# Linear attention beside a gated FFN on one core: the state gram with its operands exchanged, and the state turned by DMA

## The chip, the cores and the metric

One core of one Trainium2 chip. The metric is the device time of one execution in microseconds (us), the median of several. Executions of one kernel agree mostly within 0.3%. A run is compared only with runs of the kernel before that were made in turns with it on the same chip. The sets of runs were timed on several chips, so the ratio to the kernel before, and not the bare median, compares one set with another. Runs with a lowered clock of TensorE throughout are set aside.

## The reference

Two branches over x (2048 tokens, 640 features) are mixed by a gate per token. Branch A is linear attention with 32 heads of 20 features. Its keys and queries go through a feature map of two softmaxes, so each head has 40 features: 20 of "plus" and 20 of "minus" sign.

```python
pk = einsum("bhsd,hdf->bhsf", k, w_phi)
phi_k = concatenate([softmax(pk), softmax(-pk)], axis=-1)      # and phi_q likewise
kv  = einsum("bhsf,bhsd->bhfd", phi_k, v)                      # the state, per head 40 x 20
z   = einsum("bhsf->bhf", phi_k)
num = einsum("bhqf,bhfd->bhqd", phi_q, kv)                     # the numerators
den = einsum("bhqf,bhf->bhq", phi_q, z) + 1e-6
a   = (num / den) @ wo
b   = (gelu(x @ w_gate) * (x @ w_up)) @ w_down                 # branch B, F = 1728
out = g * a + (1 - g) * b
```

The change concerns `kv` and `z`. v carries a column of ones for each head, so one matrix product gives both; it is called the state gram below.

## The kernel before

The kernel runs in three stages: loads and weight folding (to about 23 us), a loop over 16 blocks of 128 tokens that makes keys, values and queries and adds up the gram, and the FFN in four blocks of 512 tokens. The FFN makes the hidden layer in 14 chunks (numbered 0 to 13 in the order in which they run), then the down-projection. The program gives each engine one order of instructions, and semaphores tie the engines together.

A gram pass (one per token block) makes the 128 x 128 array hold 128 key features and streams the v columns (20 + 1 per head) of the heads that those features touch. Feature tiles of 128 do not end at head borders, so a tile touches 7 or 8 heads:

```python
def gram_regions(self):            # bank -> (sign, feature tile, first head, last head)
    ...
    return {
        3: [full(0, 0), full(0, 1), full(0, 3), (1, 2, 12, 14)],
        4: [full(1, 0), full(1, 1), full(1, 3), (1, 2, 15, 17)],
        5: [full(0, 4), full(1, 4), full(0, 2), (1, 2, 18, 19)],
    }

def gram(self, t):
    ...
    n = (h1 - h0 + 1) * self.DA                                   # DA = 21
    matmul(bank(b)[:, c:c + n], Ek[:, se, s, i*P:(i+1)*P], vaug[:, sv, h0:h1+1, :], ...)
```

That is 12 matmuls a pass, 8 with 147 streamed columns, one with 168, two with 63 and one with 42: 1512 columns. After the last pass 12 VectorE multiplies take the state out of PSUM, set what belongs to no head to zero with a mask, and write it as KV, with features on the partitions. The numerators need it in that layout. The first FFN block is woven with the last passes and the first numerators:

```python
order = [0, 1, 13] + list(range(2, 13))
at = {5: 0, 8: 1, 11: 2}             # after which chunk which numerator runs
for idx, c in enumerate(order):
    self.gateup(b, c, ...)           # one chunk: ten matmuls of 512 columns
    if idx == 0: self.gram(14)
    if idx == 3: self.gram(15); self.kv_evac(); self.gates()
    if idx in at: self.num(at[idx])
```

The softmax here doesn't subtract the row's maximum and nothing guards it: scores larger than these inputs give would overflow.

Of the kernel before, what the change touches and what calls it, by code (L numbers as in the profile page):

```python
# [3 lines left out]
P = 128  # L4
BF16 = mybir.dt.bfloat16
F32 = mybir.dt.float32
AF = mybir.ActivationFunctionType
ALU = mybir.AluOpType
# [95 lines left out]
class _Kernel:  # L104
# [353 lines left out]
            sc.op("dve", lambda e, v=v, r=r: e.tensor_tensor(v, v, r, ALU.mult),  # L458
                  reads=[("Rk", se)], writes=[("Ek", se, s)])

    def gram_regions(self):
        lo = self.HLO
        full = lambda s, i: (s, i, lo[i], self.HHI[i])
        return {
            3: [full(0, 0), full(0, 1), full(0, 3), (1, 2, 12, 14)],
            4: [full(1, 0), full(1, 1), full(1, 3), (1, 2, 15, 17)],
            5: [full(0, 4), full(1, 4), full(0, 2), (1, 2, 18, 19)],
        }

    def gram(self, t):  # L470
        sc = self.sc
        se, sv = t % self.NSE, t % self.NSV
        for b, regs in self.gram_regions().items():
            c = 0
            for r, (s, i, h0, h1) in enumerate(regs):
                n = (h1 - h0 + 1) * self.DA
                sc.op("pe", lambda e, s=s, i=i, h0=h0, h1=h1, c=c, n=n, b=b, r=r: e.matmul(  # L477
                    self.bank(b)[:, c:c + n], self.Ek[:, se, s, i * P:(i + 1) * P], self.vaug[:, sv, h0:h1 + 1, :],
                    start=(t == 0 and r == 0), stop=(t == self.NT - 1 and r == len(regs) - 1)),
                    reads=[("Ek", se, s), ("vaug", sv), ("vmain", sv), ("vone", sv)], writes=[("ps", b)],  # L480
                    signal=(r == len(regs) - 1))
                c += n

    def kv_evac(self):
        sc = self.sc
        for b, regs in self.gram_regions().items():
            c = 0
            for (s, i, h0, h1) in regs:
                nh = h1 - h0 + 1
                j0 = h0 - self.HLO[i]  # L490
                dst = self.KV[:, i, s, j0 * self.DB:(j0 + nh) * self.DB].rearrange(
                    "p (h c) -> p h c", c=self.DB)[:, :, 0:self.DA]
                src = self.bank(b)[:, c:c + nh * self.DA].rearrange("p (h c) -> p h c", c=self.DA)
                m = self.mask[:, i, j0:j0 + nh].unsqueeze(2).to_broadcast([P, nh, self.DA])
                sc.op("dve", lambda e, dst=dst, src=src, m=m: e.tensor_tensor(dst, src, m, ALU.mult),
                      reads=[("ps", b), ("mask", i), ("KVd", i, s)], writes=[("KV", i, s, h0)])
                c += nh * self.DA

    def pq(self, b, i, n):
        sc = self.sc  # L500
# [149 lines left out]
    def num(self, t):  # L650
        sc = self.sc
        NBK = self.NUMB
        DB, DH = self.DB, self.DH
        old = [("xtok", k) for k in range(4)] + [("wkT", g) for g in range(6)] + [("wqT", g) for g in range(6)]
        parts = {0: [(0, 0, 6), (1, 6, 12), (2, 12, 15)], 1: [(2, 16, 19), (3, 19, 25), (4, 25, 31)]}
        kvk = {(i, s): [] for i in range(5) for s in (0, 1)}
        for regs in self.gram_regions().values():
            for (s, i, h0, h1) in regs:
                kvk[(i, s)].append(("KV", i, s, h0))
        for hf in (0, 1):  # L660
            for s in (0, 1):
                bk = NBK + 2 * hf + s
                for r, (i, h0, h1) in enumerate(parts[hf]):
                    n = (h1 - h0 + 1) * DB
                    o0 = (h0 - 16 * hf) * DB
                    k0 = (h0 - self.HLO[i]) * DB
                    sc.op("pe", lambda e, s=s, i=i, n=n, o0=o0, k0=k0, bk=bk, r=r: e.matmul(  # L667
                        self.bank(bk)[:, o0:o0 + n], self.Eq[:, s, i, t * P:(t + 1) * P],
                        self.KV[:, i, s, k0:k0 + n], start=(r == 0), stop=(r == 2), skip_group_check=True),
                        reads=[("Eq", t // 4, s, i), ("KVd", i, s)] + kvk[(i, s)], writes=[("ps", bk)],  # L670
                        signal=(r == 2))
        sl = t % 2
        N = self.ps[:, NBK * 512:(NBK + 4) * 512].rearrange("p (f s c) -> p f s c", s=2, c=512)[:, :, :, 0:16 * DB]
        V = [N[:, :, s, :].rearrange("p f (h c) -> p f h c", c=DB) for s in (0, 1)]
        Z = [v[:, :, :, DH] for v in V]
        Dn = [v[:, :, :, DH + 1] for v in V]
        R = lambda k: self.RH[:, sl, k, :, :]
        rb = [("ps", NBK + k) for k in range(4)]
        key = lambda k: ("RH", sl, k)

        def dve(fn, reads, writes, guard=()):
            sc.op("dve", fn, reads=reads, writes=writes, guard=guard)
        dve(lambda e: e.reciprocal(R(0), Dn[1]), rb, [key(0)], guard=old)  # L683
        dve(lambda e: e.tensor_tensor(R(1), Dn[0], R(0), ALU.mult), rb + [key(0)], [key(1)])
        dve(lambda e: e.tensor_tensor(R(2), Z[1], R(1), ALU.mult), rb + [key(1)], [key(2)])
        dve(lambda e: e.tensor_tensor(R(3), Z[0], R(2), ALU.add), rb + [key(2)], [key(3)])
        dve(lambda e: e.scalar_tensor_tensor(R(4), Dn[0], 1e-6, R(3), ALU.mult, ALU.add), rb + [key(3)], [key(4)])
        dve(lambda e: e.reciprocal(R(5), R(4)), [key(4)], [key(5)])
        dve(lambda e: e.tensor_scalar(R(6), R(5), self.Gr[:, t:t + 1], None, op0=ALU.mult), [key(5), "Gr"], [key(6)])
        dve(lambda e: e.tensor_tensor(R(7), R(6), R(1), ALU.mult), [key(6), key(1)], [key(7)])  # L690
        for s, dst in ((0, self.O1), (1, self.O2)):
            o = dst[:, sl, :].rearrange("p (f h d) -> p f h d", f=2, d=DH)
            f = R(6 + s).unsqueeze(3).to_broadcast([P, 2, 16, DH])
            dve(lambda e, o=o, f=f, s=s: e.tensor_tensor(o, V[s][:, :, :, 0:DH], f, ALU.mult),  # L694
                rb + [key(6 + s)], [("O", s, sl)], guard=old)
        sc.op("pool", lambda e: e.tensor_tensor(self.Og[:, sl, :], self.O1[:, sl, :], self.O2[:, sl, :], ALU.add),  # L696
              reads=[("O", 0, sl), ("O", 1, sl)], writes=[("Og", sl)], guard=old)
        gs = t % 6
        sc.dma("sp", lambda e: e.dma_start_transpose(self.goT[:, gs, :, :], self.Og[:, sl, :]),
               reads=[("Og", sl)], writes=[("goT", gs)], guard=old)  # L700
# [49 lines left out]
    def ffn(self):  # L750
        self.gn = 0
        self.pn = 0
        self.sc.op("pool", lambda e: e.memset(self.hT[0:64, 13, :], 0.0), writes=["hTz"], guard=self.oldw)
        pairs = [(6, 7), (0, 1)]
        for b in range(self.NB):
            if b == 0:
                order = [0, 1, 13] + list(range(2, 13))
                at = {5: 0, 8: 1, 11: 2}
            else:
                order = list(range(14))  # L760
                at = {2: 4 * b + 1, 6: 4 * b + 2, 10: 4 * b + 3}
            for idx, c in enumerate(order):
                if b == 0 and c == 13:
                    self.gateup(b, c, (2,))
                else:
                    self.gateup(b, c, pairs[self.pn % 2])
                    self.pn += 1
                if b == 0:
                    if idx == 0:
                        self.gram(14)  # L770
                    if idx == 3:
                        self.gram(15)
                        self.kv_evac()
                        self.gates()
                if idx in at:
                    self.num(at[idx])
            for t in range(4):
                self.down(4 * b + t, pairs[self.pn % 2])
                self.pn += 1
                if b == 0 and t == 0:  # L780
                    self.num(3)
                if b < self.NB - 1 and t == 2:
                    self.num(4 * b + 4)
# [42 lines left out]
```

## Time and profile before

| | before |
|---|---|
| median | 306.58 us (306.54 to 307.19) |
| span in the profile | 304.5 us |
| TensorE / VectorE / ScalarE busy | 97% / 53% / 35% |
| one gram pass, start to start | 0.68 us, 16 times |

From the page of the kernel before: the busy times of the engines, the clock granted to TensorE in 40 slices of the span (9 is 90% or more of full speed), and the chain of work that ended last, by engine.

```profile
PE 296.6 (97%) x2002; PEld 175.0 (57%) x2028; DVE 162.3 (53%) x317; ACT 105.2 (35%) x186; POOL 30.0 (10%) x61
PEclk9999999999999999999999999999999999999999
PE 90%; SPq 4%; DMA 3%; ACT 1%; issue 1%; DVE 0%; DVEq 0%; ACTq 0%
```

PE is TensorE, PEld its weight loads. The chain is nine tenths matmul; the rest of it is the loading phase at the start. So what is taken from TensorE's stream after that phase comes off the time, as long as nothing new makes TensorE wait.

The gram's matmuls by shape (line, engine, operation, operands, count; busy us and mean ns of one; idle time before them):

```profile
L477 PEld LDWEIGHTS ps<-vaug,Ek 128*128 128x128 bf16 x192 | 12.3, 97 | 1.8
L477 PE MATMUL ps<-vaug,Ek 128*128 128x147 bf16 x128 | 11.8, 227 | 0.0
L477 PE MATMUL ps<-vaug,Ek 128*128 128x63 bf16 x32 | 6.1, 191 | 0.0
```

The means (227 ns, 191 ns) are latencies: matmuls overlap, and a mean says nothing about what one costs in a stream. The cost is the distance from one start to the next. From the records of one pass these are, in ns: 64, 68, 66, 28, 63, 68, 66, 28, 66, 63, 72, 28, in sum 680.

The chain of waits around the last pass, in order of time (start, length, what):

```profile
98.13 0.67 PE ps L477 x12
98.81 4.32 PE ps L630 x20
103.13 0.70 PE ps L667 x12
```

L477 is the gram, L630 the gate/up chunks, L667 the first numerator. They follow each other without a gap. Two chunks (4.32 us) lie between the last gram and the first numerator; in this time VectorE makes KV.

Three lines on DMA transposes in the kernel before, one of DMA issues (count, median us from issue to landing) and two of instructions (duration min/median/max in ns). xT is 512x640 from DRAM, goT 128x640 from SBUF:

```profile
xT<-in_A_x_dram SPq DMA_TRANSPOSE x3, 5.6
L228 SPq DMA_TRANSPOSE xT<-in_A_x_dram x3: 2677/2909/2956, 9.5 to 23.5; - x3
L699 SPq DMA_TRANSPOSE goT<-Og x16: 1200/1210/1241, 109.7 to 280.8; - x16
```

### The profile page before, as it was taken

To read this page: it belongs to the slowest core of one execution; us is meant where nothing else is said; L and a number is where in the kernel's file an instruction comes from. 1 tells how busy PE (TensorE), PEld (TensorE's weight loads), DVE (VectorE), ACT (ScalarE), POOL (GpSimd) and SP (SyncE) were. 2 spreads that over 40 slices of the span, in tenths; PEclk is the share of its full clock that TensorE was granted. 3 is DMA by queue.
4 is the path that set the end of the run, shared out by engine and by line. 5 is a ranking of instruction groups with operands and counts; after the bars stand their busy time and mean duration, and the time that the engine had idled before them with its cause. 6 is when DMAs were issued, how large, how long until landed. Compare 5 with 4: busy or idle time off the path is not lost.

```text
span 304.5 us, 5031 instructions
## 1 busy us (share of the span) xinstructions
PE 296.6 (97%) x2002; PEld 175.0 (57%) x2028; DVE 162.3 (53%) x317; ACT 105.2 (35%) x186; POOL 30.0 (10%) x61
## 2 busy tenths in 40 slices
PE   8989999999999999999999999999999999999996
PEld 3656565655555555777545567754457765545763
DVE  1438999986775877234367710435770044567000
ACT  3356776667673222111322211123221122222111
POOL 7200000000000011111011000101110010111000
PEclk9999999999999999999999999999999999999999
DMA  7679994000000011120110111011001001110101
GB/s 242 176 123 248 368 366 156 2 0 0 2 0 2 0 23 25 22 65 23 44 24 0 22 24 43 24 43 23 18 6 43 24 25 43 22 22 2 43 24 43
DMA packets 33043, 18.29 MB, mean 60 GB/s; under 512 B 25147, under 2 KB 32124, under 8 KB 33020
## 3 DMA queue, kind: packets, MB, share of 16 engines
q1 hardware_dynamic: 32368, 17.95, 21.6%
q8 instruction: 16, 0.26, 0.4%
q10 hardware_dynamic: 652, 0.03, 0.1%
q14 instruction: 7, 0.06, 0.1%
HBM read 9.78 MB, written 2.62 MB: 41 GB/s over the span
## 4 chain that ended last, share of the span: by engine, by line
PE 90%; SPq 4%; DMA 3%; ACT 1%; issue 1%; DVE 0%; DVEq 0%; ACTq 0%
PE ps L630 36%; PE ps L712 20%; PE ps L371 11%; PE ps L718 7%; PE ps L503 6%; PE ps L667 4%; PE ps L477 4%; SPq L233 2%; DMA w_49<-in_A_wqkv_dram 2%; PE ps L640 1%; DMA wqT<-in_A_wqkv_dram 1%; SPq L228 1%; SPq L218 1%; ACT Eq L509 1%; PE ps L351 0%
## 5 line engine op out<-in xcount | busy, mean ns | idle before, releaser
L630 PE MATMUL ps<-xT,wu_sb 128*128 128x512 bf16 x253 | 64.2, 379 | 0.8 <-ACT Eq L509 0.2
L712 PE MATMUL ps<-wd_sb,hT 128*128 128x320 bf16 (+2 forms) x447 | 63.5, 299 | 0.1
L630 PE MATMUL ps<-xT,wg_sb 128*128 128x512 bf16 x252 | 63.0, 379 | 0.2
L633 ACT ACTIVATE gl<-ps 128x512 bf16<-128x512 f32 x52 | 31.0, 597 | 83.3 <-PE ps L630 74.2
L635 DVE TENSOR_TENSOR hT<-ps,gl 128x512 bf16<-128x512 f32 x52 | 35.7, 688 | 42.9 <-PE ps L630 42.9
L712 PEld LDWEIGHTS ps<-wd_sb,hT 128*128 128x128 bf16 x448 | 43.1, 98 | 18.2 <-DVE hT L635 0.4
L630 PEld LDWEIGHTS ps<-xT,wu_sb 128*128 128x128 bf16 x260 | 25.4, 98 | 31.1 <-issue 0.7
L630 PEld LDWEIGHTS ps<-xT,wg_sb 128*128 128x128 bf16 x260 | 24.9, 98 | 26.9
L371 PE MATMUL ps<-w_49,xT 128*128 128x512 bf16 (+3 forms) x216 | 39.0, 328 | 0.2
L696 POOL TENSOR_TENSOR Og<-O_57,O_58 128x640 bf16<-128x640 bf16 x16 | 22.3, 1393 | 167.9 <-DVE O_58 L694 167.9
L728 ACT ACTIVATE outsb<-ps,Gm 128x640 bf16<-128x640 f32 (+2 forms) x17 | 13.0, 762 | 74.1 <-PE ps L718 74.1
L371 PEld LDWEIGHTS ps<-w_49,xT 128*128 128x128 bf16 x220 | 20.8, 97 | 18.2
L683 DVE RECIPROCAL RH<-ps 128x32 f32<-128x32 f32 x16 | 5.7, 358 | 43.9 <-PE ps L667 42.8
L449 DVE TENSOR_REDUCE Dk<-Ek 128x64 f32<-128x1280 bf16 x16 | 23.7, 1482 | 7.4 <-ACT gcol L441 7.4
L458 DVE TENSOR_TENSOR Ek<-Ek,Dk 128x640 bf16<-128x640 bf16 x32 | 25.0, 822 | 0.6
L718 PE MATMUL ps<-wo_sb,goT 128*128 128x320 bf16 (+2 forms) x160 | 24.5, 299 | 0.0
L503 PE MATMUL ps<-xT,wq_50 128*128 128x512 bf16 x94 | 23.4, 378 | 0.7 <-ACT Eq L509 0.3
L509 ACT ACTIVATE Eq<-ps 128x512 bf16<-128x512 f32 x40 | 21.8, 607 | 5.8 <-PE ps L503 5.8
L438 ACT ACTIVATE Ek<-ps 128x640 bf16<-128x640 f32 x32 | 20.7, 704 | 4.1 <-PE ps L371 3.1
L718 PEld LDWEIGHTS ps<-wo_sb,goT 128*128 128x128 bf16 x160 | 15.5, 98 | 6.3
L667 PEld LDWEIGHTS ps<-KV,Eq 128*128 128x128 bf16 x192 | 12.0, 98 | 3.1
L667 PE MATMUL ps<-KV,Eq 128*128 128x154 bf16 x192 | 13.7, 221 | 0.0
(73 smaller groups left out, 183.2 us busy)
## 6 DMA issues: line engine op xcount, KB each, us to landing
out_dram<-outsb SPq DMA_DIRECT2D x15, 160.0 KB, 1.8
wd_sb<-in_B_w_down_dram SPq DMA_DIRECT2D x1, 2080.0 KB, 12.6
w_49<-in_A_wqkv_dram SPq DMA_DIRECT2D x5, 320.0 KB, 5.2
wg_sb<-in_B_w_gate_dram SPq DMA_DIRECT2D x1, 1120.0 KB, 6.5
wu_sb<-in_B_w_up_dram SPq DMA_DIRECT2D x1, 1120.0 KB, 9.0
wg_sb<-in_B_w_gate_dram SPq DMA_DIRECT2D x1, 960.0 KB, 8.9
wu_sb<-in_B_w_up_dram SPq DMA_DIRECT2D x1, 960.0 KB, 9.3
wo_sb<-in_A_wo_dram SPq DMA_DIRECT2D x1, 800.0 KB, 10.3
```

Source lines behind the costliest of these rows:

```text
L371: sc.op("pe", lambda e, kt=kt: e.matmul(self.bank(bank)[:, bcol:bcol + n], self.xT[:, kt, t * P:(t + 1) * P], self.w3[:, kt, self.D + c0:s ...
L449: sc.op("dve", lambda e: e.tensor_reduce(self.Dk[:, se, 0, :].rearrange("p (s h) -> p s h", h=H), self.Ek[:, se, :, :].rearrange("p s (h d ...
L458: sc.op("dve", lambda e, v=v, r=r: e.tensor_tensor(v, v, r, ALU.mult), reads=[("Rk", se)], writes=[("Ek", se, s)])
L503: sc.op("pe", lambda e, kt=kt: e.matmul(self.bank(bank), self.wq2[:, kt, i * P:(i + 1) * P], self.xT[:, kt, b * self.BT:(b + 1) * self.BT] ...
L509: sc.op("act", lambda e, s=s, scale=scale: e.activation(self.Eq[:, s, i, b * self.BT:(b + 1) * self.BT], self.bank(bank), AF.Exp, scale=sc ...
L630: sc.op("pe", lambda e, kt=kt, w=w, bk=bk: e.matmul(self.bank(bk), w[:, kt, c * P:(c + 1) * P], xs(kt), start=(kt == 0), stop=(kt == self. ...
L633: sc.op("act", lambda e: e.activation(self.gl[:, slot, :], self.bank(banks[0]), AF.Gelu_apprx_tanh), reads=[("ps", banks[0])], writes=[("g ...
L635: sc.op("dve", lambda e: e.tensor_tensor(self.hT[:, c, :], self.bank(banks[1]), self.gl[:, slot, :], ALU.mult), reads=[("ps", banks[1]), ( ...
L667: sc.op("pe", lambda e, s=s, i=i, n=n, o0=o0, k0=k0, bk=bk, r=r: e.matmul(self.bank(bk)[:, o0:o0 + n], self.Eq[:, s, i, t * P:(t + 1) * P] ...
L696: sc.op("pool", lambda e: e.tensor_tensor(self.Og[:, sl, :], self.O1[:, sl, :], self.O2[:, sl, :], ALU.add), reads=[("O", 0, sl), ("O", 1, ...
L712: sc.op("pe", lambda e: e.matmul(self.bank(bk, w), self.hT[:, c, tt * P:(tt + 1) * P], self.wd_sb[:, c, w0:w0 + w], start=(c == 0), stop=F ...
L718: sc.op("pe", lambda e: e.matmul(self.bank(bk, w), self.goT[:, gs, k, :], self.wo_sb[:, k, w0:w0 + w], start=False, stop=(k == self.KD - 1 ...
```

## The change

The operands of the gram are exchanged. v of six heads (126 of 128 columns) stays in the array, and the keys of these heads, both signs, are streamed: five matmuls of 240 columns and one of 80 a pass, 1280 columns in place of 1512, and 6 matmuls in place of 12. The price is that the state comes out with v on the partitions and features along the columns. So after the last pass it is copied from PSUM to SBUF (into two planes, in key buffers that are free by then), turned by two DMA transposes of 128 x 1280, and masked from SBUF in ten VectorE multiplies. To cover this longer way, the masks stand after chunk 5 and the numerators move from chunks 5, 8, 11 to 7, 10, 12.

```diff
-    def gram_regions(self): ...
+    def gram_groups(self):
+        fe = 6 * self.DH
+        for g in range(6):
+            lo = min(6 * g * self.DA, self.H * self.DA - P)
+            yield g, 3 + g % 2 if g < 4 else 5, 2 * fe * (g // 2 if g < 4 else g - 4), lo, fe * g, min(fe, self.D - fe * g)
     def gram(self, t):
-        ... matmul(bank(b)[:, c:c + n], Ek[:, se, s, i * P:(i + 1) * P], vaug[:, sv, h0:h1 + 1, :], ...)
+        for g, b, c, lo, f0, nf in self.gram_groups():
+            ... matmul(bank(b)[:, c:c + 2 * nf], va[:, lo:lo + P], Ek[:, se, :, f0:f0 + nf], ...)
     def kv_evac(self):
-        ... tensor_tensor(KV part, PSUM, mask, mult)                     # 12 times
+        ... copy(Ek[:, pl, ...], PSUM)                                   # 3 on VectorE, 1 on ScalarE
+        for pl in (0, 1):
+            dma_start_transpose(Ek[:, 2 + pl, ...], Ek[:, pl, ...])
+    def kv_mask(self):
+        ... tensor_tensor(KV part, Ek[:, 2 + g % 2, ...], mask, mult)    # 10 times, SBUF to SBUF
-                at = {5: 0, 8: 1, 11: 2}
+                at = {7: 0, 10: 1, 12: 2}
+                    if idx == 5:
+                        self.kv_mask()
```

More of the change, by code (lines that the diff above doesn't have):

```diff
@@ L459, in k_norm @@
                   reads=[("Rk", se)], writes=[("Ek", se, s)])
-    def gram_regions(self):
-        lo = self.HLO
-        full = lambda s, i: (s, i, lo[i], self.HHI[i])
-        return {
-            3: [full(0, 0), full(0, 1), full(0, 3), (1, 2, 12, 14)],
-            4: [full(1, 0), full(1, 1), full(1, 3), (1, 2, 15, 17)],
-            5: [full(0, 4), full(1, 4), full(0, 2), (1, 2, 18, 19)],
-        }
+    def gram_groups(self):
[3 more added lines that the diff above has]
+            yield g, 3 + g % 2 if g < 4 else 5, 2 * fe * (g // 2 if g < 4 else g - 4), lo, fe * g, min(fe, self.D - fe * g)
     def gram(self, t):
@@ L472, in gram @@
         se, sv = t % self.NSE, t % self.NSV
-        for b, regs in self.gram_regions().items():
-            c = 0
-            for r, (s, i, h0, h1) in enumerate(regs):
-                n = (h1 - h0 + 1) * self.DA
-                sc.op("pe", lambda e, s=s, i=i, h0=h0, h1=h1, c=c, n=n, b=b, r=r: e.matmul(
-                    self.bank(b)[:, c:c + n], self.Ek[:, se, s, i * P:(i + 1) * P], self.vaug[:, sv, h0:h1 + 1, :],
-                    start=(t == 0 and r == 0), stop=(t == self.NT - 1 and r == len(regs) - 1)),
-                    reads=[("Ek", se, s), ("vaug", sv), ("vmain", sv), ("vone", sv)], writes=[("ps", b)],
-                    signal=(r == len(regs) - 1))
-                c += n
+        va = self.vaug[:, sv, :, :].rearrange("p h c -> p (h c)")
@@ L484, in kv_evac @@
+        for g, b, c, lo, f0, nf in self.gram_groups():
+            sc.op("pe", lambda e: e.matmul(
+                self.bank(b)[:, c:c + 2 * nf], va[:, lo:lo + P], self.Ek[:, se, :, f0:f0 + nf],
+                start=(t == 0 and g in (0, 1, 4)), stop=(t == self.NT - 1 and g in (2, 3, 5)), skip_group_check=True),
+                reads=[("Ek", se, 0), ("Ek", se, 1), ("vaug", sv), ("vmain", sv), ("vone", sv)], writes=[("ps", b)],
+                signal=(g in (2, 3, 5)))
     def kv_evac(self):
@@ L485, in kv_evac @@
         sc = self.sc
-        for b, regs in self.gram_regions().items():
-            c = 0
-            for (s, i, h0, h1) in regs:
-                nh = h1 - h0 + 1
-                j0 = h0 - self.HLO[i]
-                dst = self.KV[:, i, s, j0 * self.DB:(j0 + nh) * self.DB].rearrange(
-                    "p (h c) -> p h c", c=self.DB)[:, :, 0:self.DA]
-                src = self.bank(b)[:, c:c + nh * self.DA].rearrange("p (h c) -> p h c", c=self.DA)
-                m = self.mask[:, i, j0:j0 + nh].unsqueeze(2).to_broadcast([P, nh, self.DA])
-                sc.op("dve", lambda e, dst=dst, src=src, m=m: e.tensor_tensor(dst, src, m, ALU.mult),
-                      reads=[("ps", b), ("mask", i), ("KVd", i, s)], writes=[("KV", i, s, h0)])
-                c += nh * self.DA
+        fe = 6 * self.DH
@@ new lines, in copy @@
+        def copy(ek, dst, src, rd, wr):
+            if ek == "d":
+                sc.op("dve", lambda e: e.tensor_copy(dst, src), reads=rd, writes=wr)
+            else:
+                sc.op("act", lambda e: e.activation(dst, src, AF.Copy), reads=rd, writes=wr)
+        for pl, ek in ((0, "d"), (1, "a")):
+            f = pl * fe
+            dst = self.Ek[:, pl, :, 0:4 * fe].rearrange("p s (b c) -> p b s c", c=2 * fe)[:, :, :, f:f + fe]
+            src = self.bank(3 + pl, 4 * fe).rearrange("p (b s f) -> p b s f", f=fe, s=2)
+            copy(ek, dst, src, [("ps", 3 + pl)], [("Ek", pl, 0)])
@@ new lines, in kv_evac @@
+        for pl, ek in ((0, "d"), (1, "d")):
+            g = 4 + pl
+            nf = min(fe, self.D - fe * g)
+            src = self.bank(5)[:, pl * 2 * fe:pl * 2 * fe + 2 * nf].rearrange("p (s f) -> p s f", f=nf)
+            copy(ek, self.Ek[:, pl, :, fe * g:fe * g + nf], src, [("ps", 5)], [("Ek", pl, 1)])
+        for pl in (0, 1):
+            sc.dma("sp", lambda e: e.dma_start_transpose(
+                self.Ek[:, 2 + pl, :, :].rearrange("p s (i c) -> p (s i) c", c=P),
+                self.Ek[:, pl, :, :].rearrange("p s f -> p (s f)")),
+                reads=[("Ek", pl, 0), ("Ek", pl, 1)], writes=[("Ek", 2 + pl, 0), ("Ek", 2 + pl, 1)])
@@ new lines, in kv_mask @@
+    def kv_mask(self):
+        sc = self.sc
+        self.kvk = {i: [] for i in range(self.KD)}
+        lows = {g: lo for g, b, c, lo, f0, nf in self.gram_groups()}
+        for i in range(self.KD):
+            for g in range(self.HLO[i] // 6, self.HHI[i] // 6 + 1):
+                h0, h1 = max(self.HLO[i], 6 * g), min(self.HHI[i], 6 * g + 5)
+                nh, j0 = h1 - h0 + 1, h0 - self.HLO[i]
+                o = i * P + h0 * self.DA - lows[g]
+                dst = self.KV[:, i, :, j0 * self.DB:(j0 + nh) * self.DB].rearrange(
+                    "p s (h c) -> p s h c", c=self.DB)[:, :, :, 0:self.DA]
+                src = self.Ek[:, 2 + g % 2, :, o:o + nh * self.DA].rearrange("p s (h c) -> p s h c", c=self.DA)
+                m = self.mask[:, i, j0:j0 + nh].unsqueeze(1).unsqueeze(3).to_broadcast([P, 2, nh, self.DA])
+                sc.op("dve", lambda e: e.tensor_tensor(dst, src, m, ALU.mult),
+                      reads=[("Ek", 2 + g % 2, 0), ("mask", i), ("KVd", i, 0), ("KVd", i, 1)], writes=[("KV", i, g)])
+                self.kvk[i].append(("KV", i, g))
@@ L655, in num @@
         parts = {0: [(0, 0, 6), (1, 6, 12), (2, 12, 15)], 1: [(2, 16, 19), (3, 19, 25), (4, 25, 31)]}
-        kvk = {(i, s): [] for i in range(5) for s in (0, 1)}
-        for regs in self.gram_regions().values():
-            for (s, i, h0, h1) in regs:
-                kvk[(i, s)].append(("KV", i, s, h0))
         for hf in (0, 1):
@@ L669, in num @@
                         self.KV[:, i, s, k0:k0 + n], start=(r == 0), stop=(r == 2), skip_group_check=True),
-                        reads=[("Eq", t // 4, s, i), ("KVd", i, s)] + kvk[(i, s)], writes=[("ps", bk)],
+                        reads=[("Eq", t // 4, s, i), ("KVd", i, s)] + self.kvk[i], writes=[("ps", bk)],
                         signal=(r == 2))
```

## The prediction

> **What bounds the kernel now.** The page of the profile shows TensorE busy for 97% of a 304.5 us span at a granted clock of 1.000, and the chain of waits is 90% TensorE. From about 23 us on that chain is nearly unbroken matmul. Matmul time removed after 23 us comes off the run, unless a new wait appears.
>
> **What is removed.** The state gram is 16 passes of 12 matmuls, 1512 streamed columns each. The records, start to start, give 680 ns a pass: 147 columns take 64 to 68 ns, 63 columns 28, 168 columns 72. All lie on the chain (3.5% of it). The new pass has 6 matmuls with 1280 columns (five of 240, one of 80). Interpolating this trace (320 columns take 136 ns, 147 take 66, 63 take 28) gives 103 ns and 36 ns, 552 ns a pass. The Trainium skill, "TensorE: Matmul & The Clock Gate", section "Wait — 56ns, not 53.3ns?", has N/2.4 + 2.5 ns start to start; the trace agrees (512 columns: 216 ns). Saved: 128 ns a pass, **2.05 us** in all. Fewer weight loads give nothing extra: they overlap. Every gram's operands were ready ahead (by 0.44 us at the tightest pass, 4.6 us late in the loop), so no wait arises there.
>
> **What is added, and where.** After the last gram: three VectorE copies and one ScalarE copy from PSUM (estimates from a 640-column cast at 821 ns: 0.65 + 0.4 + 0.25 us, ScalarE 0.6), two DMA transposes of 128x1280, then ten masking multiplies from SBUF (about 2.2 us, as the old twelve took 2.43). The transposes are doubtful: a 128x640 one occupies the queue 1.21 us and lands 2.6 us after issue; a 512x640 one takes 2.7 and 5.6. I estimate 1.7 to 2.4 us of queue each and the second landing 5 to 7 us after the first issue.
>
> **How much lies on the chain.** Counting from the last gram's end: copies done at 1.4 us, transposes landed at 6.4 to 8.5, masks done at 8.6 to 10.7. TensorE has four gate/up chunks of 2.16 us before it wants the first numerator: 8.64 us. The move of the numerators from chunks 5, 8, 11 to 7, 10, 12 nearly hides the new chain; I expect a stall of 0 to 2 us there, 0.6 us the most likely. VectorE, in order, sits in the masks' wait with two hidden-layer products behind it; their PSUM pairs are wanted about 2 us later, so no second stall. The tighter numerators (4.3 us apart, against 3.6 us of VectorE work each plus two products of 0.69) just fit.
>
> **Prediction.** 306.6 - 2.05 + 0.6 = **305.1 us**, 304.3 to 306.6 in 8 of 10 cases. Faster by over 2%: 0.01; within 2%: 0.975; slower by over 2%: 0.015.
>
> **What would show it.** Right: gram passes of about 0.55 us; TensorE busy 2 us less; transposes landing 5 to 7 us after the first issue; at the first numerator an idle TensorE below 2 us, released by a masking multiply. Wrong: passes of 0.6 us or more (the streamed operand has two pieces, or the weight load binds at shorter gaps); a wait of TensorE on the keys' normalising in the loop; a wait of the second or third numerator, or of the down-projection.
>
> **What would make it wrong.** A 128x1280 transpose costing far more than twice a 128x640 one: each extra microsecond goes into the stall. Or no stall at all: 304.5.

## The result and the profile after

| | before | after |
|---|---|---|
| median | 306.58 us (306.54 to 307.19) | 304.19 us (304.03 to 305.05) |
| ratio of fast runs | | 0.9923 (0.9900 to 0.9945) |
| span in the profile | 304.5 us | 302.2 us |
| one gram pass | 680 ns | 548 ns |
| from the start of the first pass to the end | 272.70 us | 270.63 us |

A ratio is the mean time of one kernel's fast runs over that of the other's in the same rounds, so it is not quite the ratio of the medians. The measured median lies 0.1 us below the low end of the predicted range: the change gave more than was predicted. A repeat of the same kernel (below) has 304.42, inside the range.

The same three lines of the page, after:

```profile
PE 294.5 (97%) x1907; PEld 172.7 (57%) x1932; DVE 163.2 (54%) x318; ACT 105.8 (35%) x187; POOL 30.0 (10%) x61
PE 90%; SPq 4%; DMA 3%; ACT 1%; issue 1%; ACTq 0%
```

TensorE is busy for 2.1 us less; VectorE and ScalarE for 0.9 and 0.6 us more, off the chain. No record of the granted clock was kept of this execution; but its 512-column matmuls start 215 to 216 ns apart, as in the kernel before at full clock. The gram by shape:

```profile
L472 PE MATMUL ps<-Ek,vaug 128*128 128x240 bf16 x80 | 10.7, 266 | 0.1
L472 PEld LDWEIGHTS ps<-Ek,vaug 128*128 128x128 bf16 x96 | 9.3, 98 | 2.1
L472 PE MATMUL ps<-Ek,vaug 128*128 128x80 bf16 x16 | 3.2, 199 | 0.0
```

Start to start one pass now has 103, 102, 103, 102, 103, 35 ns. Sixteen times 132 ns is 2.11 us, and from the first gram pass to the end the kernel is 2.08 us shorter. The gram is the whole gain there.

The chain after the last pass:

```profile
96.03 0.55 PE ps L472 x6
96.58 4.75 PE ps L651 x22
101.33 0.05 issue
101.38 3.83 PE ps L651 x17
105.21 0.69 PE ps L684 x12
```

Four chunks (L651), then the numerator (L684): no wait. What ran beside them, in order of time (start, length, engine, line; in brackets the idle time before and what ended it):

```profile
97.79 2.87 SPq L498 DMA_TRANSPOSE Ek<-Ek  x2
101.54 0.41 DVE L516 TENSOR_TENSOR KV<-Ek,mask 128x252 bf16<-128x252 bf16 x1
102.79 2.02 DVE L516 TENSOR_TENSOR KV<-Ek,mask 128x42 bf16<-128x42 bf16 x9 [0.84 <-DMA Ek<-Ek]
105.05 0.85 PE L684 MATMUL ps<-KV,Eq 128*128 128x154 bf16 x12
```

The last mask ends at 104.81 us and the first numerator starts at 105.05. Counted from the end of the last gram pass (96.41): transposes issued at 1.38, landed at 4.89 and 6.36, masks done at 8.41, wanted at 8.63. The new chain is hidden with a quarter of a microsecond to spare. And the transposes themselves (count; duration in the queue; landing):

```profile
L498 SPq DMA_TRANSPOSE Ek<-Ek x2: 1346/1356/1367, 97.8 to 99.3; - x2
Ek<-Ek SPq DMA_TRANSPOSE x2, 3.5
```

1.36 us in the queue for twice the size of one that takes 1.21 us.

### The profile page after: what moved, and what is told of

The parts are those of the page before. It is cut to its first block, busy times and chain, and to the rows that moved or that the text cites. A ratio compares the mean times of both kernels' runs of the same rounds, so it can differ in the third digit from the quotient of the medians.

```text
span 302.2 us, 4855 instructions
## 1 busy us (share of the span) xinstructions
PE 294.5 (97%) x1907; PEld 172.7 (57%) x1932; DVE 163.2 (54%) x318; ACT 105.8 (35%) x187; POOL 30.0 (10%) x61
## 4 chain that ended last, share of the span: by engine, by line
PE 90%; SPq 4%; DMA 3%; ACT 1%; issue 1%; ACTq 0%
PE ps L651 37%; PE ps L729 20%; PE ps L371 11%; PE ps L735 7%; PE ps L524 6%; PE ps L684 4%; PE ps L472 3%; SPq L233 2%; DMA w_49<-in_A_wqkv_dram 2%; PE ps L661 1%; DMA wqT<-in_A_wqkv_dram 1%; SPq L228 1%; SPq L218 1%; ACT Eq L530 1%; PE ps L351 0%
## 5 line engine op out<-in xcount | busy, mean ns | idle before, releaser
L651 PE MATMUL ps<-xT,wu_sb 128*128 128x512 bf16 x254 | 64.3, 379 | 0.7 <-ACT Eq L530 0.2
L651 PE MATMUL ps<-xT,wg_sb 128*128 128x512 bf16 x250 | 62.8, 379 | 0.4
L651 PEld LDWEIGHTS ps<-xT,wu_sb 128*128 128x128 bf16 x260 | 25.4, 98 | 31.1 <-issue 0.7
L651 PEld LDWEIGHTS ps<-xT,wg_sb 128*128 128x128 bf16 x260 | 24.9, 98 | 26.9
L684 PEld LDWEIGHTS ps<-KV,Eq 128*128 128x128 bf16 x192 | 12.0, 98 | 3.1
L684 PE MATMUL ps<-KV,Eq 128*128 128x154 bf16 x192 | 13.7, 221 | 0.0
```

Source lines behind the costliest of these rows:

```text
L651: sc.op("pe", lambda e, kt=kt, w=w, bk=bk: e.matmul(self.bank(bk), w[:, kt, c * P:(c + 1) * P], xs(kt), start=(kt == 0), stop=(kt == self. ...
L684: sc.op("pe", lambda e, s=s, i=i, n=n, o0=o0, k0=k0, bk=bk, r=r: e.matmul(self.bank(bk)[:, o0:o0 + n], self.Eq[:, s, i, t * P:(t + 1) * P] ...
```

## The experiments

My theory after the result: the time follows TensorE's stream alone. A pass costs what its columns cost, and the new chain costs nothing as long as it ends before the first numerator. Rivals: the gain comes from having half the matmuls and weight loads; or part of it from the numerators' new places; or the chain has far more room than the trace shows.

The start of the first gram pass varied between 31.6 and 34.7 us among the eleven fast profiles of kernels that have the same instructions up to there (31.76 before, 31.58 after, 31.92 and 33.44 in two more). That spread belongs to the loading phase of a run. So beside the times I give the stretch from the start of the first pass to the end, read from the records of the one profiled execution.

| run | edit | median us | ratio to before (95%) | pass, ns | first pass to end, us |
|---|---|---|---|---|---|
| before | | 306.58 | 1 | 680 | 272.70 |
| after | | 304.19 | 0.9923 (0.9900 to 0.9945) | 548 | 270.63 |
| again | none | 304.42, fast runs | 0.9926 (0.9910 to 0.9943) | | |
| sched_only | before, numerators later | 306.59 | 0.9993 (0.9980 to 1.0007) | 680 | 272.58 |
| twelve_halves | 12 matmuls, 1280 columns | 305.37 | 0.9978 (0.9945 to 1.0011) | 578 | 271.06 |
| six_wide | 6 matmuls, 1512 columns | 306.13 | 0.9978 (0.9961 to 0.9994) | 645 | 272.18 |
| num6 | numerators at 6, 9, 12 | 306.53 | 0.9997 (0.9969 to 1.0025) | 548 | 272.27 |
| num5 | numerators at 5, 8, 11 | 310.63 | 1.0126 (1.0097 to 1.0155) | 548 | 276.57 |
| one_plane_num6 | one transpose, 6, 9, 12 | 304.74 | 0.9931 (0.9912 to 0.9951) | 548 | 271.37 |
| four_transposes | both done twice | 308.29 | 1.0056 (1.0032 to 1.0080) | 548 | 274.67 |
| one_plane | one transpose | 304.11 | 0.9923 (0.9898 to 0.9947) | 548 | 270.56 |
| col64 | gram in half-array tiles | 303.83 | 0.9904 (0.9885 to 0.9923) | 419 | 269.82 |
| col64_batched | and in four stretches | 300.97 | 0.9823 (0.9804 to 0.9842) | 328 | |
| after_batched | after, in four stretches | 304.43 | 0.9933 (0.9918 to 0.9949) | 548 | |

All twelve gave a correct result. In the two batched kernels the first pass comes later, so the last column does not apply to them. Their pass is a stretch of four divided by four; for col64_batched that is an estimate, as the record of the first matmul after each stretch is missing (227 ns are taken off for it, as measured in col64).

### again: how large the gain is

No edit: the changed kernel once more.

> The changed kernel once more, unedited, timed in turns with the kernel before on the same chip, to fix the size of the gain. My theory (the gain is the shorter gram pass and nothing else, 16 x 132 ns = 2.1 us): 2.1 us less than the kernel before, 304.5. Rival (there is a further gain of 0.2 to 0.3 us somewhere, as the medians 306.58 and 304.19 say): 2.4 us less, 304.2. In the profile the start of the first gram pass tells whether the 0.18 us by which it came earlier (31.58 for 31.76) belongs to the kernel or to the run.

The profiled execution fell into a slow state (347.4 us, granted clock 0.852) and is not used. The five others have a median of 304.42, the ratio is 0.9926, a gain of 2.2 us by medians. So the gain is 2.1 to 2.4 us, and the runs do not tell these apart. In the two profiled executions of the first comparison the spans differ by 2.25 us, of which 0.18 is the earlier start of the first pass. This run's slow profile cannot say to whom that start belongs; the spread among the eleven profiles gives it to the run.

### sched_only: the new places of the numerators alone

```diff
# against the kernel before
-                at = {5: 0, 8: 1, 11: 2}
+                at = {7: 0, 10: 1, 12: 2}
```

> The kernel before, with only the numerators moved from chunks 5, 8, 11 to 7, 10, 12. My theory: TensorE does the same work in another order and never waited for the old places, so within 0.1 us of the kernel before. Rival (the new places of the numerators give the missing 0.2 to 0.3 us): 0.2 us or more faster than the kernel before.

306.59 against 306.65 in the same rounds. Moving the numerators gives nothing. It is there to cover the new chain.

### twelve_halves and six_wide: columns or number of matmuls

```diff
# twelve_halves, against the changed kernel: one matmul per sign
-            matmul(bank(b)[:, c:c + 2 * nf], va[:, lo:lo + P], Ek[:, se, :, f0:f0 + nf], ...)
+            for s in (0, 1):
+                matmul(bank(b)[:, c + s * nf:c + (s + 1) * nf], va[:, lo:lo + P], Ek[:, se, s, f0:f0 + nf], ...)
# six_wide, against the changed kernel: 252 columns in each, the extra ones not used
-            matmul(bank(b)[:, c:c + 2 * nf], va[:, lo:lo + P], Ek[:, se, :, f0:f0 + nf], ...)
+            w0 = min(f0, self.D - 126)
+            matmul(bank(b)[:, c:c + 252], va[:, lo:lo + P], Ek[:, se, :, w0:w0 + 126], ...)
```

> The changed kernel with each gram matmul cut into two, one per sign: twelve matmuls and twelve weight loads a pass as in the kernel before, but 1280 columns. My theory (streamed columns set the pass, the number of matmuls only adds some 3 ns each): ten of 120 columns at 53 and two of 40 at 28 ns or so, a pass of 580 to 590 ns, 0.55 to 0.65 us slower than the changed kernel. Rival (the gain came from halving the matmuls and weight loads): a pass near 680 ns and about 2.1 us slower, as slow as the kernel before.

> The changed kernel with the gram's streamed operand widened from 240 (last one 80) to 252 columns, with results not used in the extra ones: six matmuls a pass, but 1512 columns as in the kernel before. My theory (columns set the pass): six at 107.5 ns, 645 ns a pass, 1.55 us slower than the changed kernel. Rival (number of matmuls and weight loads): the pass stays near 550 ns and the time does not move.

Start to start, twelve_halves has 52 and 53 ns for 120 columns and 28 and 25 for 40; six_wide has 107 and 108 ns for 252 columns. Together with before and after this is a table of two by two:

| pass, ns | 1512 columns | 1280 columns |
|---|---|---|
| 12 matmuls | 680 | 578 |
| 6 matmuls | 645 | 548 |

Fewer columns bring 97 to 102 ns, fewer matmuls (with their weight loads, which these runs do not separate) 30 to 35. The expectation for twelve_halves (580 to 590) was a little high, that for six_wide exact. The stretch from the first pass to the end follows the passes: against the kernel before, six_wide is 0.53 us shorter (16 x 35 = 0.56) and twelve_halves 1.64 (16 x 102 = 1.63). The confidence intervals of the times are wide here. Two of the six executions of twelve_halves took 307.7 and 308.1 us; in the first of them, the profiled one, the clock was at half for 3.4 us from 25 us on, before the first pass, and that pass came late, at 34.7 us. The second has the same mean clock, 0.994 against 0.993. The four others have a median of 305.1, 0.7 us above the changed kernel in the same rounds (again, 304.42); six_wide is 1.7 above it. The records carry the verdict more sharply than the medians.

The Trainium skill, "TensorE: Matmul & The Clock Gate", section "Wait — 56ns, not 53.3ns?", has N/2.4 + 2.5 ns from start to start and a floor of about 25 ns. For 252, 240 and 120 columns that is 107.5, 102.5 and 52.5 ns; the trace agrees with all three, and the shortest distance seen with the whole array is 25. The 147-column matmuls of the kernel before are the exception: 65.5 ns on average where the formula gives 63.75. What these 2 ns are stays open; over eight matmuls they are some 14 of the 35 ns by which 680 exceeds 645.

### num6 and num5: how much room the chain has

```diff
# against the changed kernel
-                at = {7: 0, 10: 1, 12: 2}
+                at = {6: 0, 9: 1, 12: 2}        # num6
+                at = {5: 0, 8: 1, 11: 2}        # num5
```

> The changed kernel with the numerators after chunks 6, 9, 12 in place of 7, 10, 12. In the changed kernel's trace the masks were done 8.4 us after the last gram pass ended, and TensorE wanted the first numerator at 8.64. Now it wants it at 6.48. My theory (the chain of copies, transposes and masks was hidden with only a quarter of a microsecond to spare, and what is not hidden is paid in full): a stall of 8.4 - 6.48 - 0.4 (the last masks are needed only for the last third of the numerator's matmuls) = 1.5 us, released by a masking multiply, and 1.5 us slower than the changed kernel. Rival (there was much more room than the trace's waits show): no change.

> The changed kernel with the numerators at their old places, after chunks 5, 8, 11. My theory: TensorE wants the first one 4.32 us after the last gram, so it stalls 8.4 - 4.32 - 0.4 = 3.7 us and the whole gain is lost: about 1.5 us slower than the kernel before. Rival: as fast as the changed kernel, because later waits take the stall up.

num6: the first pass to the end is 1.64 us longer than in the changed kernel (1.5 expected; by the medians 2.1 to 2.3, with executions from 305.65 to 307.56), and the waits of its TensorE (who waited for whom: us, times, longest) name the masks:

```profile
PEld ps L684 <- DVE KV L516: 1.7, 4, 0.6
PE ps L684 <- DVE KV L516: 0.7, 3, 0.3
```

num5 came out 5.9 us longer where 3.7 was expected. Its stall is as the theory says. These are TensorE's instructions in order of time (start, length, engine, line, count; in brackets the idle time before and what ended it):

```profile
104.00 0.23 PE L684 MATMUL ps<-KV,Eq 128*128 128x154 bf16 x1 [2.24 <-DVE KV L516]
104.44 0.23 PE L684 MATMUL ps<-KV,Eq 128*128 128x154 bf16 x1 [0.21 <-DVE KV L516]
104.92 0.67 PE L684 MATMUL ps<-KV,Eq 128*128 128x88 bf16 x6 [0.26 <-DVE KV L516]
105.82 0.40 PE L684 MATMUL ps<-KV,Eq 128*128 128x154 bf16 x4 [0.22 <-DVE KV L516]
106.27 1.64 PE L651 MATMUL ps<-xT,wg_sb 128*128 128x512 bf16 x4
107.70 2.34 PE L651 MATMUL ps<-xT,wu_sb 128*128 128x512 bf16 x5
109.84 1.30 PE L651 MATMUL ps<-xT,wg_sb 128*128 128x512 bf16 x5
```

The numerator could have ended at 102.29 (the last gram's end at 97.28, two chunks of 2.16 us, 0.69 for the numerator); it ended at about 106.06, a stall of 3.8 us. (The chunk after it shows four matmuls of five: the record of the first is missing, so the line at 106.27 starts one matmul late.) But look at the sixth line: five matmuls that take 1.24 us elsewhere took 2.34. The busy times of these two stretches (length, then PE, PEld, DVE, ACT, POOL busy with counts, granted clock, DMA share, GB/s):

```profile
97.28:106.27 8.99, 5.98 (x36) 2.82 (x35) 5.79 (x20) 1.76 (x3) 0.00 (x0) 1.00 0.39 73
106.27:110.00 3.73, 3.73 (x10) 1.37 (x10) 3.25 (x10) 0.60 (x1) 0.00 (x0) 0.54 0.00 0
```

After the stall the granted clock was 0.54 on average; its records say half speed for 3.4 us from 106.5 on. Nine matmuls that start there took 3.63 us in place of 1.94: 1.7 us more. Up to the first down-projection matmul the run is then 5.45 us behind the changed kernel, and 3.8 + 1.7 is that. The rest begins with a wait there, for the hidden layer, that the changed kernel does not have (who waited for whom: us, times, longest):

```profile
PE ps L729 <- DVE hT L656: 0.3, 1, 0.3
```

The run loses 0.5 us from this point on. So the stall was paid once as waiting, once more, in part, as a slow clock afterwards, and a little as a later wait. In num6 (a stall of 1.6 us, its idle gaps 0.8 us in all) the clock did not fall, and the stall cost its own length.

### one_plane_num6 and one_plane: one transpose in place of two

```diff
# against the changed kernel: all head groups into plane 0, for each feature column belongs to one group
-            dst = self.Ek[:, pl, :, 0:4 * fe]...          # and Ek[:, pl, :, fe * g:fe * g + nf]
+            dst = self.Ek[:, 0, :, 0:4 * fe]...           # and Ek[:, 0, :, fe * g:fe * g + nf]
-        for pl in (0, 1):
+        for pl in (0,):                                   # the transpose
-                src = self.Ek[:, 2 + g % 2, :, o:o + nh * self.DA]...
+                src = self.Ek[:, 2, :, o:o + nh * self.DA]...
```

> The numerators after chunks 6, 9, 12 and only one transpose of 128x1280: the copies put all six head groups into one plane, for each feature column belongs to one group only, so one plane holds all that the masks keep. My theory: the second transpose was what the masks waited for; without it the queue's second 1.44 us go, the masks end at about 7.4 us after the last gram, and the stall is 7.4 - 6.48 - 0.4 = 0.5 us: about 1 us faster than the run with two transposes at these places, and 0.5 us slower than the changed kernel. Rival (the masks' own time and VectorE's order bound the chain, not the second transpose): the same as with two transposes.

> The changed kernel with one transpose in place of two, numerators where the changed kernel has them (7, 10, 12). My theory: the masks end some 0.8 us sooner, nobody waits for them, the time stays that of the changed kernel, within 0.15 us. Rival (something of the chain was still paid at the first numerator): faster by up to 0.3 us.

The two planes of the change are not needed: the rows of the turned plane that belong to another head group are set to zero by the mask in any case. With one transpose the masks ended 7.59 us after the last gram in place of 8.41, although the copies, now all into one plane, ended 0.3 us later. At places 6, 9, 12 this brought the stretch from 272.27 to 271.37 (0.9 us; 1 was expected), 0.74 above the changed kernel (0.5 was expected). At places 7, 10, 12 it left 270.56 against 270.63: nothing. So the second transpose was part of what the masks waited for, and at the change's own places nobody waits.

### four_transposes: three and a half microseconds more of chain

```diff
# against the changed kernel
-        for pl in (0, 1):
+        for pl in (0, 1, 0, 1):                           # the transpose
```

> The changed kernel with both transposes done twice over, the result the same. My prediction on record said that each extra microsecond of transposes goes into the stall. My theory: the fourth lands some 3.5 us after the second did (two more of 1.44 us in the queue, and each waits for the landing of the one whose output it overwrites), the masks end about 3.5 us later, at 11.9 us after the last gram, TensorE stalls 11.9 - 8.64 - 0.4 = 2.9 us: 2.9 us slower than the changed kernel, 0.8 slower than the kernel before. Rival (transposes lie off the chain by far more): no change.

The fourth transpose landed 9.92 us after the last gram (6.36 in the changed kernel), the masks ended at 11.96, both as expected to a tenth. Two of the instructions in order of time:

```profile
106.48 2.02 DVE L516 TENSOR_TENSOR KV<-Ek,mask 128x42 bf16<-128x42 bf16 x9 [1.03 <-DMA Ek<-Ek]
106.83 0.23 PE L684 MATMUL ps<-KV,Eq 128*128 128x154 bf16 x1 [1.50 <-DVE KV L516]
```

The stretch grew by 4.05 us, not 2.9. Here too the granted clock went to half for 3.4 us, from 107.6 on, though the longest single gap of TensorE was 1.50 us. The numerator could have ended at 105.87 and ended at 109.05. Some 0.15 of these 3.2 us is slow clock already (an estimate: the matmuls from 107.76 on took 1.29 us, the same ones in num5, at full clock, 1.13), and the five matmuls after it took 2.06 us in place of 1.08. So about 3.0 us are stall, as expected, and 1.1 us slow clock.

The mean clocks of the executions bear on whether the long stall brings the slow spell. One spell of 3.4 us at half speed lowers the mean over 305 us to 0.994. All four executions of num5 have 0.987 to 0.994. Of four_transposes three have 0.993 or 0.994 and took 308.23 to 309.24 us; one has 0.999 and took 307.71 us, the least. All four of num6 have 1.000. Of the other fast executions only the two slower ones of twelve_halves are so low. So the spell came in seven of the eight executions of the two kernels whose stall is 3 us or more. The length of one gap does not decide it: in the loading phase an idle gap of 1.36 us cost no clock in six_wide, while one of 1.28 us stands before the spell of twelve_halves.

### col64, col64_batched, after_batched: a faster version

The two-by-two table says that columns are the cost. Of the array's output only a sixth is kept (each head against its own features). The array can be worked in two halves of 64 columns, each with its own v and its own streamed keys: three heads (63 of 64 columns) stationary, 120 columns streamed, eleven matmuls a pass that alternate between the halves.

```diff
# col64, against the changed kernel
-        for g, b, c, lo, f0, nf in self.gram_groups():
-            matmul(bank(b)[:, c:c + 2 * nf], va[:, lo:lo + P], Ek[:, se, :, f0:f0 + nf], ...)
+        for j, b, c, lo, f0, nf in self.gram_groups():    # eleven groups of three heads
+            q = 64 * (j % 2)
+            matmul(ps[q:q + 64, b * 512 + c:b * 512 + c + 2 * nf], va[:, lo:lo + 64], Ek[:, se, :, f0:f0 + nf],
+                   tile_position=(0, q), ...)
# and copies by halves of the partitions, one transpose, eleven masks
```

> An attempt at a faster version: v of three heads stationary (63 of 64 columns), eleven matmuls a pass of 120 streamed columns (the last 80), alternating between the left and the right 64 columns of the array; the state then needs one transpose. The Trainium skill, TensorEngine Tiling (Array Packing), section Key Properties, says that tiles execute weight loads and matmuls in parallel but that a change of tiling mode drains the engine. If two halves run at once: 6 x 52 ns = 0.31 us a pass plus two drains of unknown size, so between 0.35 and 0.5 us and 1 to 3 us faster than the changed kernel. If they run one after the other: 10 x 52 + 36 = 0.56 us plus drains, as slow as the changed kernel or slower. My bet is the first, weakly, because half-width weight loads may set the pace.

Start to start one pass has 4, 74, 4, 48, 4, 49, 4, 48, 4, 49 ns: the second matmul of a pair starts 4 ns after the first, and a pair costs 52 ns, what one of them would cost alone. The halves do run at once. By shape:

```profile
L474 PE MATMUL ps<-Ek,vaug 128*64 128x120 bf16 x160 | 7.1, 220 | 0.0
L474 PEld LDWEIGHTS ps<-Ek,vaug 128*64 128x64 bf16 x176 | 5.5, 109 | 4.7 <-issue 2.3 <-DVE Ek L458 1.9 <-DVE Dk L453 0.4
```

But the stretch is only 0.8 us shorter than the changed kernel's, where 1 to 3 was expected. The distances around a pass tell why. From the last matmul before a pass to its first it is 203 ns where the changed kernel has 110 (309 where it has 216), and a pass that is followed by other work lasts 419 ns where one that is followed by another pass lasts 292. So a pass costs some 0.09 us on entry and 0.14 on leaving (127 ns, and 10 ns more at the matmul after it). The Trainium skill, "TensorEngine Tiling (Array Packing)", section "Key Properties", says that a change of tiling mode drains TensorE; it gives no figure. If these are the drains, they come off with the number of changes: these passes stand in 15 stretches, each between other work.

```diff
# col64_batched, against col64 (after_batched, against the changed kernel)
-    NSE = 4                                   # buffers of normalised keys
+    NSE = 8
-    # gram(0), then at each block t the passes up to t - 3 (t < 8) or t - 2
+    # at t = 6, 10, 14 the four passes up to t - 3
-        if idx == 0: self.gram(14)
-        if idx == 3: self.gram(15)
+        if idx == 3: self.gram(12); self.gram(13); self.gram(14); self.gram(15)
```

> The version in half-array tiles, with the sixteen gram passes gathered into four stretches of four (after the first, second and third third of the key loop and after chunk 3), for which the keys get eight buffers in place of four. In the half-array run a pass took 0.29 us where two passes stood side by side, but each stretch of passes cost about 0.09 us more on entry and 0.14 us on leaving, 15 times. My theory (those are the switches of tiling mode): eleven stretches fewer save 11 x 0.23 = 2.5 us, so some 2.5 us faster than the half-array version, 3.3 faster than the changed kernel, 301.0. Rival (the extra time belongs to each pass, not to the change of mode): no faster than the half-array version.

> The changed kernel (whole-array gram, two transposes) with the same gathering of passes and eight key buffers. My theory: no change of mode to save and no wait to remove, so within 0.2 us of the changed kernel, 304.3. Rival (gathering helps by itself, for instance through the keys' buffers): as large a gain as in the half-array version, 2 us or more.

col64_batched took 300.97 us, as expected to a tenth: 1.8% less than the kernel before and 3.2 us less than the changed kernel (medians). Against col64 it gains 2.9 us by the medians, 2.5 by the ratios, and 2.2 in the two traces from the first query matmul to the end (273.44 and 271.26 us); 2.5 was expected. after_batched took 304.43, so gathering alone gives nothing. The gain of gathering belongs to the changes between whole-array and half-array work. That a drain is what each of them costs is the page's word; the trace shows only the time.

## Why the prediction was right or wrong

The measured 304.19 us lies 0.9 below the predicted 305.1 and just below the range. The mechanism was right, and one term of the sum was mis-sized: the transposes, and with them the stall. That term is 0.6 of the 0.9 us. The remaining 0.3 is no larger than the spread between sets of runs: the repeat, with 304.42, is 0.2 slower and inside the range, so on which side of its low end the median fell was partly chance.

- "What bounds the kernel": right. From the first pass to the end the time moved by 2.08 us where TensorE's passes gave 2.11.
- "552 ns a pass", "2.05 us in all": right (548 ns, 2.11 us). The interpolation erred by 1 ns per matmul.
- "Fewer weight loads give nothing extra": nearly right. twelve_halves shows 30 ns a pass for six more matmuls with their loads, which the interpolated durations had already counted.
- No wait on the keys' normalising: right.
- "copies done at 1.4 us": right (1.38).
- **"1.7 to 2.4 us of queue each", "the second landing 5 to 7 us after the first issue", and with them "0.6 us" of stall: wrong, and this is the step that failed.** The transposes took 1.36 us of queue each, and the second landed 4.98 us after the first issue. I had placed them between a 128x640 transpose from SBUF (1.21 us) and a 512x640 one from DRAM (2.7 to 3.0 us), which differ in source as well as in size; no run separates the two. Twice the size from SBUF cost 0.15 us more in the queue. So the masks ended at 8.41 us and not at 8.6 to 10.7, before the 8.64 at which they were wanted; the stall was 0 and not 0.6. num6 and num5 show that the rest of this step was right: where the chain ends later than it is wanted, TensorE waits for the masks by about the difference.
- The range was too narrow on that side. "Or no stall at all: 304.5" was named as a possibility, with 0.2 us below it; the loading phase alone moves the start of the first pass by more than that from run to run.
- "each extra microsecond goes into the stall": right for the stall, too small for the time. four_transposes lost about 1.1 us more than its stall of 3.0, all of it in the slow spell, and num5 2.2 us more than its stall of 3.8: 1.7 in the slow spell and 0.5 from a later wait on.
- The numerators two chunks apart "just fit": right, no wait there.

## What to carry to other kernels

Cost a matmul by its streamed columns, from start to start, and choose which operand streams by counting columns; an awkward output layout may be mended off the critical path if the order of work leaves room, and the room can be read from the trace (the stalls expected from it came out within 0.15 us in num6, num5 and four_transposes). When output blocks on a diagonal are all that is kept, half-array tiles halve the stream, but only if the passes are gathered so that the mode is changed rarely. Do not scale a DMA's cost from one of another source and shape. A stall of TensorE can be dearer than its length: here 1.6 us cost 1.6, but 3.0 and 3.8 us cost 4.1 and 5.9.

## What the Trainium skill lacked or had wrong

- "TensorEngine Tiling (Array Packing)", section "Key Properties": a change of tiling mode drains TensorE, without a figure. Here changing to 128x64 tiles and back cost about 0.09 us on entry and 0.14 on leaving; eleven stretches fewer took 2.2 us off in the traces and 2.5 by the ratios (11 x 0.23 = 2.5).
- The same page, section "Restrictions", says that column tiling does without fast weight load, and does not say what that costs; elsewhere the skill has only a general factor for the fast load, none for a half-width one. The record of a 64-column load lasts 109 ns here, that of a 128-column one in the whole array 98. It did not set the pace: a pair of 120-column matmuls took 52 ns with both its loads.
- "TensorE: Matmul & The Clock Gate", section "HAM oscillation — how this bites in real kernels", gives as the rule no idle gaps of more than about 3.4 us. Here the clock went to half for 3.4 us in three profiled executions with shorter gaps: longest 2.24 us (num5) and 1.50 us (four_transposes), with further short ones right after, and 1.28 us (twelve_halves). In num6, with gaps of 0.8 us in all, and after 1.36 us in six_wide it did not. The section after that one does name frequent short pauses as a second way to lose the clock; what is lacking is how much idle time is enough.
- "DMA: Bandwidth & Descriptors" has a bandwidth for DMA transposes on this chip, and no time for a single one. Here 128x640 took 1.21 us of queue and landed after 2.6 us, 128x1280 took 1.36 and 3.5.
